# A written-out order for all steps of a chunked RWKV-7 and SiLU kernel, in place of a list scheduler's

## The chip, the cores and the metric

The kernel runs on one core of one Trainium2 chip, as one launch. The time is device microseconds of that core, median over runs. Engines are named as in the profile: PE (TensorE matmul) and PEld (its weight loads), DVE (VectorE), ACT (ScalarE), POOL (GpSimd), SP (SyncE, which issues most of the DMAs).

## The reference

Two blocks follow each other. The first is a recurrence over 768 tokens for 4 batches and 8 heads, with a state of 40 by 40 for each; the second is a feed-forward layer on the recurrence's output.

```python
for t in range(S):                     # r, k, v, w, a, b: (4, 8, 768, 40) float32
    y[:, :, t] = np.einsum('bhd,bhde->bhe', rt, state)
    Sa = np.einsum('bhde,bhe->bhd', state, at)
    state_decay = state * wt[:, :, None, :] - np.einsum('bhd,bhe->bhde', Sa, bt)
    state = state_decay + np.einsum('bhd,bhe->bhde', vt, kt)
x = y.transpose(0, 2, 1, 3).reshape(3072, 320)
h = x @ w_in                           # (320, 2048)
return (h * (1.0 / (1.0 + np.exp(-h)))) @ w_out    # w_out: (2048, 320), both weights float64
```

## The kernel before

The 768 tokens are cut into 12 chunks of 64. Inside a chunk the recurrence is written as products of small matrices and one triangular inverse per head and batch; between chunks only the state `G` is handed on. For chunk n the code lays down groups of steps:

- `load(n)`, `load_r(n)`: DMAs of w, b, a, k, v, and of r and v again.
- `prepare(n)`: on DVE two scans over w (`down`, `up`; L627, L645), the products that make `kb` and `a` (L664, L654); on PE the products of all keys with `a` (`between`, L682), transposes (`turn`, L769) and `sv` (L744); on ACT the copies out of PSUM (`sb` L407, `kt` L782, `R` L756).
- the inverse. For the first three chunks it is `special(n)`: small diagonal blocks go through DRAM (`ms`) to `xs`, DVE inverts them step by step (`dots`, L795 and L796), the result comes back through DRAM (`zs`) to `mi`, and PE and DVE alternate in three rounds (`more`, L958 on PE, L973 on DVE). For the later chunks it is `inverse(k)`, two chunks at a time on DVE, and `merge(n)` (L1039, L1068 on PE).
- `chain(n)`: the state's path. `right` (L1111), `solve` (L1135), `solve_t` (L1166), `turn` (L1196), `update` (L1223), with DVE's L1121 and L1239 between them.
- `read(n)`: the chunk's output y. `look` (L1269) and its masking on DVE (L1281), `write_state` (L1308), `write` (L1323), `scaled` (L1334).
- `moe(n)`: the feed-forward layer on the chunk's 256 rows. `full` (L1405) and `rest` (L1418) fill four PSUM tiles, ACT applies SiLU (L1428), `second` (L1445) multiplies by `w_out`, DVE copies out (L1457).

Once, at the start, `weights(i)` for i from 0 to 9 turns the float64 weights into float32 by bit operations: DMAs from POOL's queue (L479), then steps on DVE (L484, L486, L487, L493, L500), ACT (L485, L488, L502) and, for the first three, sums on PE (`sum_`, L508) and a product on DVE (L520).

Every group calls `plan.add(engine, cost, do, r, w, pri, rooms, k, size, shape)`, which only records a step: its engine, an estimated cost, the steps that it must follow (from the keys it reads and writes), and the PSUM or SBUF tiles ("rooms") that it takes from a small pool, four PSUM tiles `pair` and two SBUF tiles `lam`. There are 1449 steps: 383 on PE, 391 on DVE, 223 on ACT, 21 on POOL, 431 on SP. `shape` is a letter for the form of a PE step's matmuls: F for the full array of 128 by 128 (`full`, `second`, `sum_`), R for `rest`, Q for the 64-wide small products, T for transposes, H for `write` and `update`, S for `merge`.

The order in which the steps are emitted is the order of the instructions in each engine's queue, and each engine takes its queue strictly in that order. `plan.best(10, 400)` searches for it: a list scheduler (`order`) places the steps one by one by estimated times and priorities, a second model (`through`) rates the whole order, and 410 settings of the priorities are tried with a fixed random seed. Then the steps are emitted:

```python
    with tc.manual_schedule():
        for op in plan.best(10, 400):
            op["do"]()
```

Of the kernel before, what the change touches and what calls it, by code (L numbers as in the profile page):

```python
# [33 lines left out]
class Plan:  # L34
# [4 lines left out]
    def __init__(self, slots):  # L39
        self.slots = slots  # L40
        self.free = {k: [(0.0, i) for i in range(len(v))] for k, v in slots.items()}
        self.ops, self.wrote, self.read = [], {}, {}
# [23 lines left out]
    HOP = {"SP": 0.1, "ACT": 0.15, "PE": 0.15, "DVE": 0.15, "POOL": 0.2}  # L66
    RATE, LAND = 300.0, 2.0
    COLD = 42.0
    URGE = {"SP": 0.0, "ACT": 0.03, "PE": 0.05, "DVE": 0.1, "POOL": 0.02}
    LEAVE = {"F": 0.09, "R": 0.2, "T": 0.13, "Q": 0.13, "H": 0.12, "S": 0.11}  # L70
    ENTER = {"F": 0.08, "R": 0.1, "T": 0.03, "Q": 0.03, "H": 0.03, "S": 0.03}

    def turn(self, op):

        a, b = self.shape, op["shape"]
        if a == b or {a, b} == {"R", "T"}:
            return 0.03 if a != "F" else 0.0
        return self.LEAVE[a] + self.ENTER[b]

    def walk(self, start, cost, k, keep=False):  # L80


        fetched, count, t = self.fetched[-2:], self.count, start
        step, end = cost / max(k, 1) * (2 if start < self.COLD else 1), count + k
        have = len(self.fetched)
        while count < end:
            block = count // 256
            gate = 256 * block + 194
            if have == block + 1:
                fetched.append(max(t + 0.4, fetched[-1] + 2.6) + 1.3)  # L90
                have += 1
            if count >= gate:
                t = max(t, fetched[-1] + 0.1)
            to = min(end, gate if count < gate else 256 * block + 256)
            t += (to - count) * step
            count = to
        if keep:
            self.fetched += fetched[2:]
            self.count = end
        return t  # L100

    def order(self):
        ops = self.ops
        self.fetched, self.count, self.shape = [0.0, 0.0], 0, "Q"
        nexts = [[] for _ in ops]
        for op in ops:
            op["wait"] = len(op["before"])
            for b in op["before"]:
                nexts[b].append(op)
        ready = {e: [op for op in ops if op["engine"] == e and not op["wait"]] for e in self.HOP}  # L110
        at = dict.fromkeys(self.HOP, 0.0)
        out, held = [], {}
        queue = dict.fromkeys(("SP", "ACT", "POOL"), 0.0)
        for op in ops:
            op["ready"] = 0.0
        while len(out) < len(ops):
            best = None
            for e, some in ready.items():
                starts = []
                for op in some:  # L120
                    s = max(at[e], op["ready"])
                    for room in op["rooms"]:
                        if room.slot is None:
                            free = self.free[room.kind]
                            fits = free and held.get((room.kind, room.most), 0) < room.most
                            s = max(s, min(free)[0]) if fits else 1e9
                    lost = 0.0
                    if e == "PE" and s < 1e8:
                        lost = self.walk(s + self.turn(op), op["cost"], op["k"]) - s - op["cost"]
# [3 lines left out]
                urge = self.URGE[e]  # L133
# [1526 lines left out]
```

## Time and profile before

| | before |
|---|---|
| median of 3 runs | 734.69 us (729.82 to 736.58) |
| profiled execution | 734.2 us from first to last instruction; no time outside it is shown |
| PE busy, PEld busy | 676.8 us, 542.3 us |
| DVE, ACT, POOL busy | 419.7, 194.1, 15.2 us |
| mean granted PE clock | 0.971 |
| DMA | 77.15 MB, 105 GB/s on average |

The profile gives for each engine how long it was busy, for a stretch of time how much of it each engine was busy and at which share of full speed the PE clock was granted, and for an instruction how long its engine had stood idle before it and what ended the idle time. In a row of the time line, "[4.01 <-PE pair L958]" says that the engine had been idle for 4.01 us and that PE's L958 released it. PE's records are doubled: each matmul of the program in float32 shows as two.

### The profile page before, as it was taken

To read this page: it belongs to the slowest core of one execution; us is meant where nothing else is said; L and a number is where in the kernel's file an instruction comes from. 1 tells how busy PE (TensorE), PEld (TensorE's weight loads), DVE (VectorE), ACT (ScalarE), POOL (GpSimd) and SP (SyncE) were. 2 spreads that over 40 slices of the span, in tenths; PEclk is the share of its full clock that TensorE was granted. 3 is DMA by queue.
4 is the path that set the end of the run, shared out by engine and by line. 5 is a ranking of instruction groups with operands and counts; after the bars stand their busy time and mean duration, and the time that the engine had idled before them with its cause. 6 is when DMAs were issued, how large, how long until landed. Compare 5 with 4: busy or idle time off the path is not lost.

```text
span 734.2 us, 27298 instructions
## 1 busy us (share of the span) xinstructions
PE 676.8 (92%) x12666; PEld 542.3 (74%) x12666; DVE 419.7 (57%) x614; ACT 194.1 (26%) x241; POOL 15.2 (2%) x35
## 2 busy tenths in 40 slices
PE   2179899998999999999999999999999999999995
PEld 2177568787778678878778878778777778787773
DVE  6845799977469348397364883372992676020000
ACT  3251625422302413304312305132104312102020
POOL 2101000000000000000000000000000000000000
PEclk9996999999899999999999999999997999999998
DMA  7680754751721554417355306354215033201001
GB/s 249 150 235 27 205 194 128 223 128 37 177 93 25 137 138 141 126 46 162 81 136 142 103 19 145 87 149 130 66 27 119 26 103 108 44 20 41 18 1 22
DMA packets 117921, 77.15 MB, mean 105 GB/s; under 512 B 65538, under 2 KB 114229, under 8 KB 117160
## 3 DMA queue, kind: packets, MB, share of 16 engines
q1 hardware_dynamic: 113220, 64.43, 33.5%
q0 software_dynamic: 2224, 10.63, 4.4%
q8 instruction: 101, 1.65, 0.9%
q10 hardware_dynamic: 2356, 0.26, 0.3%
q14 instruction: 20, 0.16, 0.1%
HBM read 60.29 MB, written 14.61 MB: 102 GB/s over the span
## 4 chain that ended last, share of the span: by engine, by line
PE 86%; DVE 5%; ACT 3%; issue 2%; DMA 1%; SPq 1%; ACTq 0%; DVEq 0%
PE pair L1445 30%; PE pair L1405 23%; PE pair L1418 6%; PE pair L1269 4%; PE pair L682 3%; PE pair L1323 3%; PE pair L958 2%; PE pair L1223 2%; PE pair L744 2%; PE pair L1135 2%; PE pair L1068 2%; PE pair L1308 1%; PE pair L1111 1%; PE pair L1166 1%; PE pair L508 1%
## 5 line engine op out<-in xcount | busy, mean ns | idle before, releaser
L1445 PE MATMUL pair<-wo,gts 128*128 128x320 f32 x768 | 221.6, 445 | 0.2 <-issue 0.2
L1445 PEld LDWEIGHTS pair<-wo,gts 128*128 128x128 f32 x768 | 145.7, 193 | 60.5 <-issue 4.3
L1405 PE MATMUL pair<-xt,wi 128*128 128x256 f32 x768 | 176.6, 387 | 0.2 <-DVE wi L520 0.2
L1405 PEld LDWEIGHTS pair<-xt,wi 128*128 128x128 f32 x768 | 145.6, 192 | 22.8 <-issue 1.3
L1428 ACT ACTIVATE gts<-pair 128x1024 f32<-128x1024 f32 x48 | 46.5, 1020 | 107.5 <-PE pair L1418 100.4
L1457 DVE COPY ot<-pair 128x320 f32<-128x320 f32 x24 | 11.8, 491 | 95.2 <-PE pair L1445 93.5
L682 PE MATMUL pair<-a,kb 40*64 40x64 f32 x1536 | 33.5, 241 | 33.5 <-DVE a L654 28.7
L796 DVE TENSOR_REDUCE XI<-XI 128x64 f32<-128x512 f32 (+9 forms) x85 | 58.7, 690 | 2.9
L682 PEld LDWEIGHTS pair<-a,kb 40*64 40x64 f32 x1536 | 29.7, 153 | 36.6 <-issue 18.4
L1418 PE MATMUL pair<-xt,wi 64*128 64x256 f32 x384 | 47.9, 389 | 0.0
L1418 PEld LDWEIGHTS pair<-xt,wi 64*128 64x128 f32 x384 | 35.1, 187 | 6.3 <-issue 2.0
L1334 DVE TENSOR_TENSOR lam<-pair,wz 128x1024 f32<-128x1024 f32 x11 | 13.5, 1224 | 41.6 <-PE pair L1323 41.4
L1281 DVE TENSOR_TENSOR lam<-pair,ml 128x1024 f32<-128x1024 f32 x22 | 26.5, 1220 | 14.0 <-PE pair L1269 12.4
L795 DVE TENSOR_TENSOR XI<-XI,mi 128x1024 f32<-128x1024 f32 (+8 forms) x60 | 33.7, 561 | 1.5
L1269 PEld LDWEIGHTS pair<-r,vut 40*64 40x64 f32 x1536 | 26.3, 142 | 6.4 <-issue 4.8
L1269 PE MATMUL pair<-r,vut 40*64 40x64 f32 x1536 | 29.3, 228 | 1.1 <-issue 1.1
L664 DVE TENSOR_TENSOR kb<-kbv 128x512 f32<-128x512 f32 (+1 forms) x36 | 29.8, 860 | 0.2
L1001 ACT COPY mi<-XI 128x1024 f32<-128x1024 f32 x5 | 10.1, 2023 | 70.6 <-DVE XI L796 70.6
L627 DVE TENSOR_TENSOR_SCAN kbv<-wz,zt 128x1024 f32<-128x1024 f32 x12 | 27.5, 2292 | 0.5
L645 DVE TENSOR_TENSOR_SCAN wz<-wz,zt 128x1024 f32<-128x1024 f32 x12 | 27.5, 2291 | 0.4
L795 DVE TENSOR_TENSOR XI<-XI,xs 128x1024 f32<-128x1024 f32 (+1 forms) x25 | 25.2, 1009 | 0.7
L407 ACT ACTIVATE vu<-pair 64x640 f32<-64x640 f32 x13 | 9.1, 700 | 58.8 <-PE pair L1135 56.0
(152 smaller groups left out, 686.8 us busy)
## 6 DMA issues: line engine op xcount, KB each, us to landing
wz<-in_wT SPq DMA_DIRECT2D x12, 512.0 KB
kbv<-in_bT SPq DMA_DIRECT2D x12, 512.0 KB
a<-in_aT SPq DMA_DIRECT2D x12, 512.0 KB
kbv<-in_kT SPq DMA_DIRECT2D x12, 512.0 KB
r<-in_rT SPq DMA_DIRECT2D x48, 96.0 KB
vut<-in_vT SPq DMA_DIRECT2D x48, 96.0 KB
vu<-in_v SPq DMA_DIRECT2D x24, 160.0 KB
out<-ot SPq DMA_DIRECT2D x48, 80.0 KB
```

Source lines behind the costliest of these rows:

```text
L627: nc.vector.tensor_tensor_scan(back(V), back(W[:, 2 : 2 + Q * C]), zt, 1.0, ALU.mult, ALU.add)
L645: nc.vector.tensor_tensor_scan(Z, Z, zt, 0.0, ALU.mult, ALU.add)
L664: TTn[engine].tensor_tensor(out=at_(kb, place(is_b, first), (576 * step, 4 // step), (128, 4), (1, C)), in0=blocks((kf, bf)[is_b]), in1=bl ...
L682: nc.tensor.matmul(room.tile[half(b), j, g * C : g * C + C], lhsT=kb[rows(j), place(is_b, q) : place(is_b, q) + C], rhs=A[rows(j), q * C : ...
L795: nc.vector.tensor_tensor(out=at_(tmp, 0, *dims), in0=x, in1=y, op=ALU.mult)
L796: nc.vector.tensor_reduce(out=out_, in_=at_(tmp, 0, *dims), axis=AX.X, op=ALU.add)
L1269: nc.tensor.matmul(pl.tile[half(1 - b if role else b), b, c * C : c * C + C], lhsT=vut[rows(b), role, hu, :], rhs=rs[rows(b), hh, :], star ...
L1281: lambda pl=pl, la=la: nc.vector.tensor_tensor(out=la.tile.rearrange("p (q t) -> p q t", q=Q), in0=pl.tile.rearrange("p a b -> p (a b)").r ...
L1405: nc.tensor.matmul(rooms[g].tile[:, f // 2, (f % 2) * T : (f % 2) * T + T], lhsT=wi[:, k, (4 * g + f) * 128 : (4 * g + f) * 128 + 128], rh ...
L1418: nc.tensor.matmul(rooms[g].tile[:, h, (f % 2) * T : (f % 2) * T + T], lhsT=wi3[half(h), g * 256 + (f % 2) * 128 : g * 256 + (f % 2) * 128 ...
L1428: nc.scalar.activation(out=gts[:, 4 * g * T : 4 * g * T + 4 * T], in_=rooms[g].tile.rearrange("p a b -> p (a b)"), func=AF.Silu)
L1445: nc.tensor.matmul(po[b].tile[:, 0, 0:DM], lhsT=g4[:, f, 128 * b : 128 * b + 128], rhs=wo[:, f, :], start=f == 0, stop=f == NF - 1,)
```

## The change

`order`, `through`, `best` and their constants are removed. In their place a table, `ORDER`, lists the numbers of all 1449 steps in the order in which they are emitted, and `SLOTS` gives for each room, in the order in which the rooms first appear, which of the four or two tiles it gets. `follow` assigns the tiles, asserts that every step stands behind those that it depends on, and returns the steps.

```diff
-    def order(self):
...
-    def through(self, out, crowd, rate, hop, slower):
...
-    def best(self, draws, steps):
...
+    def follow(self, order, slots):
+
         rooms = {id(room): room for op in self.ops for room in op["rooms"]}
...
+        assert sorted(order) == list(range(len(self.ops))) and len(slots) == len(rooms)
+        for room, slot in zip(rooms.values(), slots):
+            room.slot, room.tile = int(slot), self.slots[room.kind][int(slot)]
+        done = set()
+        for n in order:
+            assert self.ops[n]["before"] <= done
+            done.add(n)
+        return [self.ops[n] for n in order]
+
+ORDER = """
+0 7 3 12 1 8 10 84 2 6 116 9 13 14 11 15 16 24 19 23 20 21 22 17 18 33 34 85 128 90 117 91 92 118 4 86 119 120
...
+SLOTS = """
+03001232301203122111130320222320301111320102321113313310011210213030203110022213111112000230101001222221320121
...
-        for op in plan.best(10, 400):
+        for op in plan.follow([int(n) for n in ORDER.split()], "".join(SLOTS.split())):
```

The steps, their instructions and what each must wait for are the same as before; only their order in each queue and the tiles are other ones. In the changed file every line of the kernel stands 144 lower, so L682 is L538 there, and L1445 is L1301.

Three places show it. The first is DVE in the first chunks, from the last round of `more` for chunk 0 (L973) on. Before, `off_diagonal` of chunk 1 (L900) comes next, and the maskings of `look` for chunk 0 (L1281) stand between the first and the later `dots` of chunk 1 (L795, L796):

```order
L973 TENSOR_TENSOR X_94<-pair_111,X_94 128x4x128
L900 TENSOR_TENSOR sb_90<-sb_90,ml 128x1024
L729 TENSOR_TENSOR lam_116<-pair_113,ml 128x1024
L795 TENSOR_TENSOR XI<-ZQ,xs 128x2
L796 TENSOR_REDUCE ZQ<-XI 128x2
L795 TENSOR_TENSOR XI<-ZQ,xs 128x8
L796 TENSOR_REDUCE ZQ<-XI 128x2x2
L1281 TENSOR_TENSOR a_83<-pair_114,ml 128x1024
L1281 TENSOR_TENSOR sb_89<-pair_113,ml 128x1024
L795 TENSOR_TENSOR XI<-ZQ,xs 128x18
```

Now all `dots` of chunk 1 follow the last round of `more` (L829, once L973) without a break, and this stands behind them, from the last pair of them on:

```order
L651 TENSOR_TENSOR XI<-ZQ 128x512
L652 TENSOR_REDUCE ZQ<-XI 128x8x8
L340 TENSOR_SCALAR wi<-wo 128x2x512
L376 TENSOR_TENSOR wi_67<-wi_67,pair_114 128x1024
L1137 TENSOR_TENSOR sb_89<-pair_113,ml 128x1024
L342 SCALAR_TENSOR_TENSOR wi<-wo,wi 128x2x512
L343 TENSOR_SCALAR wo<-wo 128x1024
L1137 TENSOR_TENSOR a_83<-pair_114,ml 128x1024
L756 TENSOR_TENSOR sb_90<-sb_90,ml 128x1024
```

So the maskings (L1137, once L1281) and `off_diagonal` of chunk 1 (L756, once L900) moved behind the `dots`, and weight steps (L340, L376, L342, L343) stand between them. The masking of chunk 1's `sv` (L729, now L585) and two weight steps moved ahead of the rounds of `more`.

The second place is PE's queue at the start. Before, from the fourth row on, with `prepare` of chunk 1 (L682), `special` of chunk 0 (L926, L913) and `more` (L958); the first weight sum (L508) stands only at row 22:

```order
L769 MATMUL pair_114<-ident,kb 128x40 x16
L744 MATMUL pair_111<-vu_99,lam_115 64x40 x32
L682 MATMUL pair_112<-a_84,kb 64x64 x32
L926 MATMUL pair_113<-ident,mi 128x64 x8
L926 MATMUL pair_114<-ident,mi 128x64 x8
L913 MATMUL pair_111<-mi,sb_89 64x64 x16
```

Now, from the same transpose on (L625, once L769; L769 at the end of these rows was L913):

```order
L625 MATMUL pair_113<-ident,kb 128x40 x16
L538 MATMUL pair_114<-a_83,kb 64x64 x32
L364 MATMUL pair_111<-gts,ident 128x512 x3
L538 MATMUL pair_113<-a_84,kb 64x64 x32
L364 MATMUL pair_111<-gts,ident 128x512
L538 MATMUL pair_112<-a_84,kb 64x64 x32
L769 MATMUL pair_114<-mi,sb_89 64x64 x16
```

The four sums of the first weight block (L364, once L508) and the second product of chunk 1's `prepare` moved ahead of `special`, and `sv` of chunk 0 (L744) moved behind `more`.

The third place is PE's queue in chunk 4's `second` (L1445), where the steps of chunk 5 lie between its parts. Before:

```order
L1445 MATMUL pair_111<-wo,gts 128x320 x4
L1269 MATMUL pair_113<-r,vut 64x64 x32
L769 MATMUL pair_114<-ident,kb 128x40 x16
L1445 MATMUL pair_111<-wo,gts 128x320 x4
L1323 MATMUL pair_112<-lam_115,kt_88 40x64 x16
L1323 MATMUL pair_112<-lam_116,kt_88 40x64 x16
L1039 MATMUL pair_113<-ZQ,sb_89 32x32 x32
L1445 MATMUL pair_111<-wo,gts 128x320 x4
L1068 MATMUL pair_114<-X_94,ZQ 32x32 x32
L682 MATMUL pair_112<-a_84,kb 64x64 x32
L1445 MATMUL pair_111<-wo,gts 128x320 x4
L1445 MATMUL pair_113<-wo,gts 128x320 x8
```

Now, in the same chunk (L1301 was L1445, L1179 was L1323, L538 was L682, L991 was L1135, L625 was L769, L1079 was L1223):

```order
L1301 MATMUL pair_111<-wo,gts 128x320 x4
L1179 MATMUL pair_113<-lam_116,kt_88 40x64 x16
L1179 MATMUL pair_113<-lam_115,kt_88 40x64 x16
L538 MATMUL pair_114<-a_84,kb 64x64 x32
L991 MATMUL pair_112<-R_93,X_95 64x40 x32
L625 MATMUL pair_113<-ident,kb 128x40 x16
L625 MATMUL pair_114<-ident,kb 128x40 x16
L1301 MATMUL pair_111<-wo,gts 128x320 x4
L1301 MATMUL pair_112<-wo,gts 128x320 x4
L1301 MATMUL pair_111<-wo,gts 128x320 x4
L1301 MATMUL pair_112<-wo,gts 128x320 x4
L1079 MATMUL pair_114<-vu_100,kt_88 40x40 x32
```

The small steps stand in longer groups between parts of `second`, and the parts follow each other more often, in turn for the two halves of the chunk's rows. Over the 383 steps of PE, the shape letter changes from one step to the next 242 times before and 205 times now.

More of the change, by code (lines that the diff above doesn't have):

```diff
@@ L3 @@
 from math import prod
-from random import Random
 import concourse.bass as bass
@@ L40, in __init__ @@
         self.slots = slots
-        self.free = {k: [(0.0, i) for i in range(len(v))] for k, v in slots.items()}
         self.ops, self.wrote, self.read = [], {}, {}
@@ L64, in add @@
         return op
[L66 to L100, printed above, removed]
```

177 lines of the change are left out of this document (4 added, 173 removed), and 56 rows, old and new, of the table ORDER.

## The prediction

> **What bounds the kernel now.** I read the page's shares first, then the slices, then the chain that ended last, and then the stretches in which PE is not full.
>
> ```profile
> span 734.2 us, 27298 instructions
> PE 676.8 (92%) x12666; PEld 542.3 (74%) x12666; DVE 419.7 (57%) x614; ACT 194.1 (26%) x241; POOL 15.2 (2%) x35
> PE   2179899998999999999999999999999999999995
> DVE  6845799977469348397364883372992676020000
> PEclk9996999999899999999999999999997999999998
> PE 86%; DVE 5%; ACT 3%; issue 2%; DMA 1%; SPq 1%; ACTq 0%; DVEq 0%
> ```
>
> PE is busy 92% and carries 86% of the chain. From the fifth slice (73 us) on its digits are 8 and 9 alone until the last one. So no other order can gain much there except by making the same matmuls pass faster: fewer breaks between kinds, fewer waits of under a microsecond, fewer windows at a low clock. Before that, in the first slices, PE waits. The kernel has two regimes, and I cost the new order in each.
>
> Stretches of the start, with the busy time of PE, PEld, DVE, ACT and POOL, then clock, DMA share and GB/s:
>
> ```profile
> 0.00:36.00 36.00, 7.43 (x224) 7.11 (x224) 27.29 (x61) 11.25 (x14) 7.67 (x22) 1.00 0.71 200
> 36.00:76.00 40.00, 35.22 (x969) 28.95 (x970) 21.53 (x39) 13.47 (x20) 3.72 (x7) 0.83 0.46 127
> 76.00:102.00 26.00, 23.05 (x376) 15.85 (x376) 20.50 (x24) 11.53 (x11) 1.62 (x3) 1.00 0.59 169
> 102.00:144.00 42.00, 39.28 (x802) 31.39 (x801) 39.75 (x44) 24.23 (x27) 1.06 (x2) 0.96 0.61 197
> ```
>
> From 102 to 144 us DVE is busy 39.75 of 42 us: it decodes the last weights, and PE's `second` of chunk 0 cannot end before the last block is there. So up to 144 us DVE is the bound, and what it idled earlier is what the start costs. That is 8.7 us before 36, 18.5 us from 36 to 76, 5.5 us from 76 to 102 and 2.3 us after, 35 us in all. PE takes its first step of chunk 1's `full` right after:
>
> ```profile
> 150.68 6.91 PE pair L1405 x32
> ```
>
> (The row of the chain starts 0.4 us inside that step.)
>
> **Term 1, the start.** DVE's waits in that stretch:
>
> ```profile
> 20.48 1.23 DVE L900 TENSOR_TENSOR sb<-sb,ml 128x1024 f32<-128x1024 f32 x1 [1.77 <-DMA ms<-sb]
> 43.72 0.69 DVE L973 TENSOR_TENSOR XI<-pair,X 128x512 f32<-128x512 f32 x1 [4.01 <-PE pair L958]
> 47.23 0.69 DVE L973 TENSOR_TENSOR XI<-pair,X 128x512 f32<-128x512 f32 x1 [1.88 <-PE pair L958]
> 54.42 1.23 DVE L900 TENSOR_TENSOR sb<-sb,ml 128x1024 f32<-128x1024 f32 x1 [3.62 <-DMA ms<-sb]
> 61.39 1.23 DVE L1281 TENSOR_TENSOR a<-pair,ml 128x1024 f32<-128x1024 f32 x1 [3.70 <-PE pair L1269]
> 68.78 1.29 DVE L1334 TENSOR_TENSOR X<-pair,wz 128x512 f32<-128x512 f32 x2 [2.16 <-PE pair L1135]
> 72.45 0.82 DVE L1239 TENSOR_TENSOR G<-pair,wc 128x640 f32<-128x640 f32 x1 [0.94 <-PE pair L1223]
> 81.70 1.23 DVE L486 SCALAR_TENSOR_TENSOR wi<-wo,wi 128x1024 int32<-128x1024 int32 x1 [1.52 <-ACT wi L485]
> ```
>
> Each is a step at the head of DVE's queue with work behind it that was ready. In the new queue:
>
> - 4.01 us ahead of the first L973: seven steps now stand there (two L729, L900, L520, L484, L486, L487). At 1.2 us for each of the five long ones and 0.7 for the two short ones (L486 above takes 1.23, L900 1.23) they are 7.4 us of work. The wait goes.
> - 3.62 us at L900: it waited for the DMAs that read `sb`, and held up the `dots` behind it. L900 now stands behind the `dots`. The wait goes.
> - 3.70, 2.16 and 0.94 us: `look` (L1269) and what follows it came late on PE, and DVE stood at their masking. All `dots` of chunk 1 and some weight steps are now ahead of it. The waits go, 6.8 us.
> - 1.77 us at 20 us, and others before 36: `down` of chunk 1 stands directly behind chunk 0's `prepare`, so DVE works while `sb` goes through DRAM. But the wait for `xs` comes back in another form, and I take 2 us as gained.
> - 1.52 us and the like from 76 to 102: I take 1 us of 5.5.
>
> That is 4.0 + 3.6 + 6.8 + 2 + 1 = 17.4 us. The 1.88 us and the small waits between rounds stay: there PE and DVE alternate whatever the queue. Against it stand three `dots` of chunk 2 (about 1.3 us) that moved ahead of the last weight steps, and about 1 us for `write` of chunk 0, whose masking is now later in DVE's queue than `update`. **Term 1: 17.4 - 2.3, some 15 us.**
>
> PE must follow. Two rows say that it can:
>
> ```profile
> 36.16 1.99 PE L682 MATMUL pair<-a,kb 40*64 40x64 f32 x64 [15.07 <-DVE a L654]
> 57.26 2.07 PE L508 MATMUL pair<-gts,ident 128*128 128x512 f32 x2
> ```
>
> PE stood idle for 15.07 us until chunk 1's `a`; the four sums of the first weight block (2.07 us at 57 us) now lie in that gap, and chunk 1's second product follows its first. So after `more` PE has some 10 us less ahead of chunk 0's `update`. What is behind a later instruction matters too: on ACT the second half of chunk 0's `u` (L407) now stands behind a weight step that waits for DVE's `dots`; walked through with the durations above, it comes free about when PE reaches `update`. On SP, one piece of `xt` stands behind the `ms` DMAs of chunk 2, but only `rest` reads it, after two `full` (7.11 us, row below).
>
> Bounds of the term: 24 us if all that DVE idled between 36 and 102 us goes, and 5 us if only the two L900 waits do (1.77 and 3.62) and the others come back elsewhere. I take 15, nearer to the sum of named waits.
>
> **Term 2, fewer changes of form.** Rows of the chain, each a run on PE between two other kinds:
>
> ```profile
> 286.23 3.65 PE pair L1405 x16
> 296.27 7.11 PE pair L1405 x32
> 309.20 17.43 PE pair L1445 x64
> 361.74 2.35 PE pair L1445 x8
> 388.22 1.09 PE pair L1269 x64
> 289.88 2.02 PE pair L1269 x128
> ```
>
> Two L1405 steps in one run take 7.11 us and apart 7.30, so a break costs 0.19. Two L1269 steps: 2.18 - 2.02 = 0.16. Eight L1445 steps in a run take 17.43, 2.18 each, against 2.35 alone: 0.17 to 0.2. From chunk 1's `full` to the end, the shape letter changes 197 times before and 169 times now; 28 x 0.16 = **4.5 us**. The nine other changes lie in the start, where DVE is the bound. Bounds: 3 us at 0.1 for a break that was part hidden, 6 us at 0.2.
>
> **Term 3, the clock.** Stretches at a low clock, in the same columns:
>
> ```profile
> 53.20:66.90 13.70, 13.58 (x288) 10.22 (x290) 7.50 (x18) 1.89 (x3) 0.00 (x0) 0.50 0.06 14
> 131.70:135.20 3.50, 3.50 (x8) 2.06 (x7) 3.47 (x5) 2.72 (x3) 0.00 (x0) 0.51 0.68 183
> 196.60:203.40 6.80, 6.65 (x95) 4.78 (x88) 2.60 (x5) 0.00 (x0) 0.00 (x0) 0.50 0.75 198
> 247.80:251.30 3.50, 3.50 (x32) 1.93 (x31) 0.00 (x0) 0.99 (x2) 0.00 (x0) 0.51 0.60 104
> 558.40:568.70 10.30, 9.49 (x147) 8.12 (x144) 1.39 (x2) 2.44 (x4) 0.00 (x0) 0.50 0.47 89
> ```
>
> The first two are in the start. The other three are 20.6 us at half speed, a loss of 10.3 us. What stood ahead of them:
>
> ```profile
> 195.79 1.25 PE L682 MATMUL pair<-a,kb 40*64 40x64 f32 x60 [0.92 <-issue]
> 246.31 0.69 PE L769 MATMUL pair<-ident,kb 40*128 40x40 f32 x16 [0.81 <-DVE ZQ L409]
> 557.15 0.75 PE L1039 MATMUL pair<-ZQ,sb 32*32 32x32 f32 x64 [0.72 <-DVE lam L729]
> 559.34 1.99 PE L682 MATMUL pair<-a,kb 40*64 40x64 f32 x64 [0.81 <-DVE ZQ L409]
> ```
>
> Small matmuls with gaps of under a microsecond. Counting the steps by their durations, PE has 11 stretches of over 3.4 us after chunk 1's `full` that hold no F or R step, the longest 11.5 us; the new order has 17, the longest 5.5 us. Two of the 11 (190 and 555 us) were followed by half speed, and a shorter stretch (244 us). More stretches but shorter ones: I take nearly the same loss, **2 us** less, with bounds of 10.3 gained and 10.3 lost again.
>
> [...]
>
> **Term 4, waits for other engines.** The waits at 246, 557 and 559 us come from DVE steps that PE reached too soon. In the new order at least one `full`, `rest` or part of `second` (1.9 us and up) lies between `merge`'s two products in nearly all chunks, and between `look` and `write`. I take **2 us**, with bounds of 0 and 3.
>
> "issue" waits of near 1 us, like the 0.92 above, come where small matmuls are densest: counted over PE's records, those at 168, 172, 196, 353, 357, 391 and 496 us come 194 or 195 instructions past a multiple of 256. The new order has about as many places where 256 instructions pass in under 2.4 us. Nothing, with 4 us to either side.
>
> **The sum.** 15 + 4.5 + 2 + 2 = 23.5 us from 734.2 us, 710.7 us. The median is 0.5 us above the profiled execution, so 711 us. Outside the profile nothing is added or removed: the last stretch is the same steps.
>
> **The rivals.**
>
> - *The start gains little.* The in-order queues of ACT and SP hold what DVE's queue no longer does: the L407 behind a weight step, `xt` behind the `ms` DMAs. Then term 1 is 5 us, and the time is 711 + 10 = 721, with 720 to 728 around it. For it speaks that ACT's queue has such a crossing; against it that ACT is busy only 13.47 of the 40 us from 36 to 76.
> - *The clock stays full* after the start: term 3 is 10.3 us in place of 2, and the time 711 - 8.3 = 702.7, down to 698 with the upper bound of term 2 and some of the "issue" waits gone. For it: no stretch is longer than 5.5 us. [...]
> - *Half speed in most chunks*, which is the way to a slower kernel. The 17 stretches of small steps are spread over all chunks. If one of them is followed by a phase like that at 558 us, it costs 10.3 / 2 = 5.1 us. Without any the time is 702.7, so six such phases bring back the time before, and the eighth, at 743 us, makes it slower by over 1%. Against it: of the 11 stretches before, only two had such a phase, and each held a gap of 0.8 us or more.
> - *Nothing measurable*: the waits move and the sum stays within 1%. The order rows leave no doubt that the queues change, so this needs terms that cancel.
>
> **How the numbers follow.** The forecast, 703 to 720 us, gets 0.68; the start that gains little 0.13; the full clock 0.12; half speed in most chunks 0.04; nothing measurable 0.03. A measurement of this kernel, whose runs lie between 729.82 and 736.58 us, tells about 1% from no change, so faster means under 727.3 us: 0.68 + 0.12 + 0.11 of the first rival, 0.91. Same gets 0.05, slower 0.04. The range goes from 698, the full clock with the bounds of terms 1 and 2 partly reached, to 727, the upper end of the rival on the start.
>
> **What would show it.** In the changed profile: the first `full` of chunk 1 (then L1261) at 133 to 138 us instead of 150; DVE idle some 20 us up to there instead of 35; L756 and L1137 without waits of 3 us; half speed after the start for about 18 us in all; single waits of PE for DVE after 150 us under 0.5 us. It is wrong if the start ends later than 145 us, which would show an ACT or SP crossing that I judged too small, or if phases at half speed add up to over 40 us.

## The result, and the profile after

| | before | after |
|---|---|---|
| median | 733.28 us (729.82 to 737.61, 9 runs) | 742.85 us (739.27 to 745.82, 9 runs) |
| ratio | | 1.0108 (95%: 1.0072 to 1.0144) |
| profiled execution, span | 734.2 us | 737.7 us (739.51 us with what lies around it) |

The change makes the kernel slower by 1.1% by the ratio, where 711 us was forecast, and the time lies above the predicted range of 698 to 727 us. The medians are 9.6 us apart, 1.3%; all ratios here are those on record for the fast runs, and are not quotients of the medians. The page of the changed kernel, with the rows that answer to those of before:

```profile
span 737.7 us, 27220 instructions
PE 672.7 (91%) x12666; PEld 543.0 (74%) x12666; DVE 417.9 (57%) x614; ACT 194.0 (26%) x241; POOL 16.2 (2%) x35
PE   2597989999999998999999999999999999999995
DVE  7769787984876454926275854356962454511000
PEclk9879979999999999999999999989999999999998
q8 instruction: 101, 1.65, 0.9%
PE 80%; DMA 6%; issue 5%; DVE 4%; SPq 3%; ACT 1%; ACTq 0%; DVEq 0%
```

PE's work is the same, and from the fifth slice on PE's slices are as full as before. What differs is in the last row. In the chain, DMA went from 1% to 6% and SPq, which issues DMAs, from 1% to 3%. Most of the DMA pieces lie in the start: `ms` and `xs` of chunk 1 (7.85 us from 44 us on, 3.40 from 52), `a` of chunk 2 (9.04 from 74) and v of chunk 1 (8.98 from 94). They belong to the start, which is taken up below. The share of "issue" went from 2% to 5%: in the start it grew from 9.2 to 16.8 us, and in the rest, from PE's step 65 on (see below), from 8.6 to 21.8 us. The waits of PE by what ended them show where that is. Before, from 150 to 725 us (all rows with "issue"; columns: total us, times, longest):

```profile
PE pair L682 <- issue: 2.8, 4, 0.9
PE pair L1269 <- issue: 1.1, 2, 0.6
PE pair L1308 <- issue: 0.9, 1, 0.9
PE pair L744 <- issue: 0.8, 1, 0.8
PE pair L1445 <- issue: 0.2, 1, 0.2
```

After, from 142 to 729 us (the largest six of twelve such rows; the other six add 3.8 us):

```profile
PE pair L1164 <- issue: 4.7, 3, 2.2
PE pair L600 <- issue: 3.7, 2, 2.5
PE pair L1125 <- issue: 2.9, 3, 1.4
PE pair L924 <- issue: 2.7, 3, 1.1
...
PE pair L1179 <- issue: 1.4, 2, 0.9
PE pair L769 <- issue: 1.4, 1, 1.4
```

5.8 us became 20.6 us. All of these waits stand 193 to 195 instructions past a multiple of 256 in PE's records. I take them for waits for the next block of instructions: the row "q8 instruction" above has 101 packets with 1.65 MB, 16 KB each, and PE's queue of 25,449 records (25,332 matmuls and weight loads, the rest its own waits and branches, which count in the position too) is 99.4 blocks of 256. Below they are called **block waits**. One of them on PE's time line in the changed kernel:

```profile
277.74 0.64 PE L625 MATMUL pair<-ident,kb 40*128 40x40 f32 x16
278.31 1.10 PE L1022 MATMUL pair<-X,R 64*40 64x64 f32 x64
279.24 1.09 PE L991 MATMUL pair<-R,X 64*64 64x40 f32 x64
280.14 0.64 PE L600 MATMUL pair<-vu,lam 64*64 64x40 f32 x27
283.24 1.17 PE L600 MATMUL pair<-vu,lam 64*64 64x40 f32 x37 [2.46 <-issue]
```

Three small steps in a row, each about 1 us long and 128 instructions (64 matmuls and their weight loads), and in the third PE stands for 2.46 us, in the middle of a step whose first 27 matmuls have passed. The packets of queue q8 show why. The point "194" is the instruction 194 past a multiple of 256:

```
                        last "194"   block's DMA starts   took    next "194": PE goes on
after, 283 us              278.69         280.74          0.88      283.24   (other DMAs busy 61%)
after, 408 us              404.59         405.33          1.24      408.00   (2%)
after, 572 us              569.01         569.72          1.10      572.10   (2%)
```

There are 22 such waits in this stretch, if gaps down to 0.06 us are counted. In all of them PE goes on 1.2 to 1.6 us after the block has come, and the DMA takes 0.9 to 1.5 us. It starts 0.6 to 1.1 us after the last "194" in fifteen, 1.7 to 2.1 us after it in five, among them the first row, where other DMAs are busy, and 0.3 us or less after it in two (at 627 and 672 us). So 256 instructions took 3.1 to 3.5 us in the fifteen, 4.0 to 4.8 in the five and 2.5 to 2.6 in the two, where PE's own work was 2.0 to 4.4 us. Where the block was there already, PE did not wait: from 428.40 to 430.64 us 256 instructions passed in 2.24 us, and the DMA had ended at 426.38 us.

One PE step can be compared exactly in all kernels here: where both orders have the same set of PE steps behind them. That is so at PE's steps 65, 142 and 381 (of 383). From step 65 to step 381, with every gap of PE over 0.06 us counted and half speed at half its length (at half speed the matmuls of L1301 follow each other in 533 ns in the changed kernel, at full speed in 269 ns, medians):

| worked out from the trace | before | after | difference in time |
|---|---|---|---|
| step 65 reached at | 130.9 us | 127.7 us | -3.2 |
| block waits after it | 6.6 us | 20.6 us | +14.0 |
| other waits of PE | 3.9 us | 2.0 us | -1.9 |
| stretches at half speed | 23.9 us | 20.5 us | -1.7 |
| what is left over (changes of shape: 200, 171) | | | -3.7 |
| time from step 65 to 381 | 590.6 us | 597.3 us | +6.7 |

(The 6.6 us before are the 5.8 us above and a gap of 0.77 us at 181 us, two or three instructions short of such a place. The profile puts it down to DVE, and it ended 0.67 us before the block's DMA did, so that it is a block wait is not shown.)

### The profile page after: what moved, and what is told of

It is laid out like the page before. It is cut to its first block, busy times and chain, and to the rows that moved or that the text cites. A ratio compares the mean times of both kernels' runs of the same rounds, so it can differ in the third digit from the quotient of the medians.

```text
span 737.7 us, 27220 instructions
## 1 busy us (share of the span) xinstructions
PE 672.7 (91%) x12666; PEld 543.0 (74%) x12666; DVE 417.9 (57%) x614; ACT 194.0 (26%) x241; POOL 16.2 (2%) x35
## 3 DMA queue, kind: packets, MB, share of 16 engines
q8 instruction: 101, 1.65, 0.9%
## 4 chain that ended last, share of the span: by engine, by line
PE 80%; DMA 6%; issue 5%; DVE 4%; SPq 3%; ACT 1%; ACTq 0%; DVEq 0%
PE pair L1301 29%; PE pair L1261 22%; PE pair L1274 6%; PE pair L1125 3%; PE pair L538 3%; PE pair L1179 3%; PE pair L1079 2%; PE pair L1164 2%; PE pair L924 1%; PE pair L625 1%; PE pair L600 1%; PE pair L1022 1%; DMA ms<-sb 1%; PE pair L967 1%; DMA a<-in_aT 1%
## 5 line engine op out<-in xcount | busy, mean ns | idle before, releaser
L1301 PE MATMUL pair<-wo,gts 128*128 128x320 f32 x768 | 223.1, 446 | 0.0
L1301 PEld LDWEIGHTS pair<-wo,gts 128*128 128x128 f32 x768 | 146.8, 195 | 59.5 <-issue 4.6
L1261 PEld LDWEIGHTS pair<-xt,wi 128*128 128x128 f32 x768 | 147.5, 194 | 23.8 <-issue 1.1
L1137 DVE TENSOR_TENSOR lam<-pair,ml 128x1024 f32<-128x1024 f32 x22 | 26.3, 1220 | 48.8 <-PE pair L1125 48.8
L538 PE MATMUL pair<-a,kb 40*64 40x64 f32 x1536 | 30.5, 236 | 20.1 <-DVE a L510 20.0
L538 PEld LDWEIGHTS pair<-a,kb 40*64 40x64 f32 x1536 | 27.6, 149 | 25.4 <-ACT kbv L532 14.6
L263 ACT ACTIVATE sb<-pair 128x1024 f32<-128x1024 f32 x12 | 12.3, 1027 | 60.0 <-PE pair L538 48.1
L638 ACT COPY kt<-pair 128x640 f32<-128x640 f32 x24 | 16.3, 693 | 43.8 <-PE pair L625 41.9
L1190 DVE TENSOR_TENSOR lam<-pair,wz 128x1024 f32<-128x1024 f32 x11 | 13.5, 1223 | 21.8 <-PE pair L1179 21.7
```

The source lines that it names most:

```text
L538: nc.tensor.matmul(room.tile[half(b), j, g * C : g * C + C], lhsT=kb[rows(j), place(is_b, q) : place(is_b, q) + C], rhs=A[rows(j), q * C : ...
L1137: lambda pl=pl, la=la: nc.vector.tensor_tensor(out=la.tile.rearrange("p (q t) -> p q t", q=Q), in0=pl.tile.rearrange("p a b -> p (a b)").r ...
L1261: nc.tensor.matmul(rooms[g].tile[:, f // 2, (f % 2) * T : (f % 2) * T + T], lhsT=wi[:, k, (4 * g + f) * 128 : (4 * g + f) * 128 + 128], rh ...
L1301: nc.tensor.matmul(po[b].tile[:, 0, 0:DM], lhsT=g4[:, f, 128 * b : 128 * b + 128], rhs=wo[:, f, :], start=f == 0, stop=f == NF - 1,)
```

## The experiments

Each is the whole kernel; only `ORDER` and `SLOTS` differ, or a few matmuls are added. "Old" is the order before, "new" that of the change. Ratios are to the kernel before on the same chip.

**1. The two orders crossed at step 142.** There the new order was 10.0 us ahead in the profile.

```diff
-ORDER = new
+ORDER = new up to PE's step 142, then the old order for all that is left   (new_then_old)
+ORDER = old up to PE's step 142, then the new order for all that is left   (old_then_new)
```

> The new order for PE's first 142 steps and what goes with them on the other engines, then the old order for the rest. PE has the very same 142 steps behind it at that place in both kernels, and reached it at 266.3 us in the changed profile against 276.3 before: a lead of 10.0 us. Theory 'blocks' (the new order's second part loses because small matmuls stand closer, and PE waits for the next block of 256 instructions): the second part is the old one and keeps its crossings, since the number of PE instructions ahead of it is the same, so the lead stays: 733 - 10 = 723 us, within 3 us. Rival 'debt' (the new start only pushes loads, weight steps and copies back, and pays for them later): the lead is lost again, 733 to 743 us. Rival 'clock' (half-speed phases fall by accident): anything from 715 to 735, by 3.4 us in each phase that appears or goes at half speed for 6.8 us.

> The reverse: the old order for PE's first 142 steps, then the new order. 'Blocks': without the lead and with the dense second part, 10 us above the changed kernel or 13.5 above the one before, 747 to 750 us; block waits of over 15 us after 277 us. 'Debt': the old start leaves nothing to pay, so the second part costs what it cost before, 730 to 736 us. 'Clock': between the two, with the phases at half speed elsewhere.

Measured: 736.70 us, ratio 1.0026 (0.9979 to 1.0073), and 751.29 us, ratio 1.0261 (1.0159 to 1.0364). The second time lies just above the 747 to 750 us that "blocks" gave, and the block waits after step 142 are 15.1 us, over 15 as expected. But it is no proof, because the crossing itself brings a wait that neither order has. At step 142 PE stood for 7.89 us, until DVE had the `a` of a `prepare` that it had begun only then:

```profile
277.70 1.98 PE L537 MATMUL pair<-a,kb 40*64 40x64 f32 x64 [7.89 <-DVE a L509]
```

Half speed went with it from 272.2 to 285.8 us. PE worked for 8.1 of these 13.6 us, which costs some 4 us. With both taken off, 751 us would be some 739, between the 730 to 736 of "debt" and the 747 to 750 of "blocks". The first run does not agree with "blocks", and its time lies in the range of "debt". PE came to step 142 at 268.7 us, 7.6 us ahead, and the old second part then lost it again: 9.0 us of block waits against 2.9 in the old kernel's own profile, mostly at the same steps, and 20.5 us at half speed against 10.2. One block's DMA started 2.5 us after PE had entered the block before, and PE waited for 3.1 us. So the same order pays different block waits in different executions, and a lead of 10 us in one pair of profiles is not a lead of the median. This pair of runs does not decide between "blocks" and "debt"; experiments 2, 3 and 5 do.

**2. A shift in the blocks.** Matmuls of the identity are added where PE is idle; every later step then lies further on in its block.

```diff
+                    if sums.pop('left', 0):
+                        for d in range(10):      # 48 in the other run
+                            px, py = slice(64 * (d % 2), 64 * (d % 2) + 64), slice(64 * (d // 2 % 2), 64 * (d // 2 % 2) + 64)
+                            nc.tensor.matmul(pf.tile[py, d % 2, 0:64], lhsT=ident[px, px], rhs=ident[px, px], start=True, stop=True)
                     nc.tensor.matmul(
                         pf.tile[:, h],
```

> The changed kernel with 10 matmuls of 64 by 64 (40 PE instructions, under 1 us) ahead of the first weight sum, where PE stands idle. Nothing else moves, but each later step lies 40 instructions further in the 256-instruction blocks. 'Blocks': taking the profiled stream of the changed kernel with its block waits removed, and letting each crossing come no sooner than 3.0 to 3.3 us after the one before, the waits after 142 us come to 13 to 19.5 us as it is (20.6 measured) and to 19.6 to 26.5 with 40 more: some 6.5 us slower than the changed kernel, 747 to 751 us. 'Debt' and 'clock': as the changed kernel, 739 to 746, with the waits at the same steps.

> As the last, with 48 matmuls (192 instructions, under 3 us in PE's idle time of 3.9 us). 'Blocks': by the same sum the waits come to 9.7 to 14.7 us, some 4 to 5 us less: 736 to 740 us, and some 12 us less than with 40. 'Debt' and 'clock': as the changed kernel, 739 to 746.

Measured: 734.85 us, ratio 1.0041 (0.9989 to 1.0093) with 40 instructions, and 727.37 us, 0.9907 (0.9863 to 0.9952) with 192. By the ratios that is 0.7% and 2.0% less than the changed kernel's 1.0108, some 5 and 15 us. The interval of the first overlaps the changed kernel's, that of the second does not. That 48 idle matmuls take 15 us out of the kernel is what "debt" and a fixed cost of the order cannot give; PE came to step 65 no earlier than in the changed kernel, so the gain lies behind it. My sizes were wrong, though: with 40 I had the sign wrong. The block waits after step 65 were 15.7 and 12.0 us (after: 20.6) and half speed 6.8 and 10.2 us (20.5). The first is under my sum of 19.6 to 26.5, because I let each crossing take 3.0 to 3.3 us, where the profile has some that wait for nothing: at 428 us of the changed kernel, above, the 256 instructions before had taken 13.0 us, and the block's DMA had ended 2.0 us before the 2.24 us began.

**3. The dense groups opened.** At 13 places of the new order one step of the full array moves ahead of the last small step of a group. The place of the time line above, on PE:

```diff
 L1022 MATMUL pair<-X,R x32
 L991 MATMUL pair<-R,X x32
+L1261 MATMUL pair<-xt,wi x8
 L600 MATMUL pair<-vu,lam x32
-L1261 MATMUL pair<-xt,wi x8
 L1261 MATMUL pair<-xt,wi x8
```

> The changed kernel's order, with one step of the full array (`full` or `second`) moved ahead of the last small step of a dense group, at 13 places behind chunk 1's first `full` where PE had waited 194 instructions past a multiple of 256. Every other queue keeps its order. 'Blocks': each 194th instruction then comes 3.0 us or more after the last one, and by the sum over the profiled stream the block waits fall from 20.6 us to 3 to 7; 18 more changes of shape at 0.16 us cost 2.9 us; of the half speed behind the longest waits (20.5 us) a third to a half goes, 3 to 5 us gained. 743 - 15 + 3 - 4 = 727 us, within 5. Rival 'breaks' (the prediction's own model, in which only the changes of shape count): 743 + 3 = 746 us. Rival 'debt' (the start pays back later): 743, no change.

Measured: 726.46 us, ratio 0.9888 (0.9838 to 0.9937), where 727 was expected and 746 by the prediction's own model. The same place (the lines stand one lower here):

```profile
281.83 1.10 PE L1021 MATMUL pair<-X,R 64*40 64x64 f32 x64
282.76 1.09 PE L990 MATMUL pair<-R,X 64*64 64x40 f32 x64
283.78 3.72 PE L1260 MATMUL pair<-xt,wi 128*128 128x256 f32 x16
287.43 1.14 PE L599 MATMUL pair<-vu,lam 64*64 64x40 f32 x64
289.39 3.72 PE L1260 MATMUL pair<-xt,wi 128*128 128x256 f32 x16 [0.81 <-ACT R L611]
```

The wait of 2.46 us is gone; a smaller one for ACT is the price. And from the eighth slice (127 us) on, no slice is under nine tenths of full clock, and the trace has no half speed between 127 us and the end of the work at 723 us:

```profile
PE   1488797998999999999999999999999999999995
PEclk9888998999999999999999999999999999999999
```

From step 65 to 381 this kernel takes 579.2 us, 18.1 less than the changed one: block waits 3.2 instead of 20.6 us, half speed 0 instead of 20.5 us (10.2 us of time), other waits 9.2 instead of 2.0, and 2.4 us left over for 18 more changes of shape, 0.13 each. The steps that I had counted as a gain, fewer changes of shape, are here given up with profit. That the time came out at 727 almost to the microsecond is partly luck: half speed gave back 10.2 us where 3 to 5 were expected, and the other waits took 7.2 us that were not in the sum.

**4. DMAs of r and v earlier.** Seven loads move ahead of DMAs at which SP stood.

```diff
 L448 DMA r<-in_rT 48x2x256
+L448, L457 DMA r, vut (the other seven of chunk 1)
 L555 DMA ms<-sb 16x16x16 x2
-L457, L448 (seven, between the next DMAs)
```

> The changed kernel with seven DMAs of r and v for chunk 1 moved ahead of the two DMAs of chunk 2's small blocks, at which SP stood from 76 to 88 us. In the changed profile PE waited 2.87 us for v at 103 us, in `look` of chunk 1, and 10.2 us at half speed followed, 5.1 us lost. 'SP queue': both go, chunk 1's first `full` comes at 134 to 139 us in place of 141.7, and the end with it, 735 to 740 us. Rival 'DVE bounds the start': PE then waits for DVE's weights instead, and nothing is left of it by 150 us: 741 to 745.

> Both of the last two edits. If both work by themselves, their gains add: 743 - 16 - 5 = 722 us, within 6, faster than the kernel before. If the loads do nothing, as with the 13 moved steps alone.

Measured: 743.54 us, ratio 1.0116 (1.0058 to 1.0173), and with the opened groups 729.03 us, 0.9964 (0.9924 to 1.0005). PE's wait for v went, and nothing was gained. The time is the rival's, but not its cause: from 80 to 152 us PE's longest waits were not for DVE's weights but block waits, 3.21 us at 93 us and 4.45 us at 115 us in the first of the two. The start ended no earlier; step 65 came at 134.5 and 134.3 us.

**5. The wait measured by itself.** Two trains of matmuls that wait for nothing, at the start and behind all work.

```diff
+    for d in range(640):
...
+        nc.tensor.matmul(pairs[0][py, d % 2, 0:64], lhsT=ident[px, px], rhs=ident[px, px], start=True, stop=True)
+    for d in range(320):
...
+        nc.tensor.matmul(pairs[0][py, d % 2, 0:128], lhsT=ident[px, px], rhs=ident[px, 0:128], start=True, stop=True)
     nc.tensor.matmul(pb[0:1, 0:1], lhsT=count, rhs=ones, start=True, stop=True)
```

> The changed kernel with two trains of matmuls that nothing waits for, once ahead of the first weight sum (DMAs busy) and once after all work (DMAs idle): 640 matmuls of 64 by 64 by 64, 2560 PE instructions, and 320 with 128 columns, 1280 instructions. At the profiled rate of 15.6 ns for a pass of 64 columns the first train takes 20 us, 2.0 us for each 256 instructions. 'Blocks': PE waits once in each 256 instructions and passes them in 3.0 to 3.4 us with the DMAs idle and up to 4 us with them busy, 30 to 40 us for the train; the second train, at twice the time for an instruction, has 4 us for each 256 and no waits. Rival (the waits come from tiles, semaphores or loads): no waits in either train, 20 us each. Nothing of the kernel's work is left out.

PE's time line behind all work, with the DMAs idle (128 records are 256 instructions with their weight loads):

```profile
777.46 2.09 PE L1383 MATMUL pair<-ident 64*64 64x64 f32 x128 [1.04 <-issue]
780.93 2.09 PE L1383 MATMUL pair<-ident 64*64 64x64 f32 x128 [1.38 <-issue]
784.67 2.09 PE L1383 MATMUL pair<-ident 64*64 64x64 f32 x128 [1.65 <-issue]
788.69 2.09 PE L1383 MATMUL pair<-ident 64*64 64x64 f32 x128 [1.93 <-issue]
...
811.49 16.89 PE L1386 MATMUL pair<-ident 64*64 64x128 f32 x591 [1.05 <-issue]
```

and in the start, with the DMAs busy:

```profile
24.83 2.10 PE L369 MATMUL pair<-ident 64*64 64x64 f32 x128 [0.46 <-issue]
31.03 3.69 PE L369 MATMUL pair<-ident 64*64 64x64 f32 x128 [4.10 <-issue]
38.05 3.69 PE L369 MATMUL pair<-ident 64*64 64x64 f32 x128 [3.33 <-issue]
```

256 instructions are 2.09 us of work, and PE waits once in each 256, but for one block of the start at half speed: a block takes 3.1 to 4.0 us with the DMAs idle and 3.1 to 7.0 with them busy. With 128 columns a block passes in 3.5 to 3.8 us, and 591 records pass without a wait of over 0.15 us. Tiles, semaphores and the kernel's loads of data have no part in the waits with idle DMAs. (The whole kernel with its trains took 837.31 us, in a single run.)

**6. The start, and the form.** The old start before the opened new order; the old order as a table; the load of chunk 2's `a` earlier; and two dense groups of the start opened as well.

```diff
+ORDER = old up to PE's step 65, then the new order with the 13 moved steps   (old_start_spread)
+ORDER = old                                                                   (old_table)
+ORDER = 13 moved steps; L421 DMA a<-in_aT of chunk 2 right behind L421 wz<-in_wT   (spread_early_a)
+ORDER = the last; L967 of chunk 1 behind the last L814, L1164 behind one L1261     (spread_start)
```

> The old order for PE's first 65 steps and what goes with them, then the new order with the 13 moved steps. PE has the same 65 steps behind it there in all of these kernels. It came there at 130.9 and 126.4 us in the two profiled executions that begin with the old order, and in the seven that begin with the new one at 126.5, 127.7, 130.9, 131.0, 134.3, 134.3 and 134.5. Theory 'the start gains nothing': the time is that of the 13 moved steps with the new start, 726, or up to 5 us less, 721 to 727. Rival 'the start gains its 15 us' (term 1 of the prediction): without the new start the time is 741. Rival 'a few us', as the first pair of profiles has it (3.2): 730.

> The old order and the old tiles, written out as a table: nothing but the form of the change, without its order. 'The form costs nothing': the time before, 731 to 736 us, and the profile a second sample of the old order's waits, block waits of 6 to 12 us after 150 us. If the form mattered, or if the two versions differed in anything but the order, it would lie elsewhere.

> The new order with the 13 moved steps, and one DMA more moved: the load of chunk 2's `a` (0.5 MB) stands on SP right behind that of w, three loads and a few small DMAs earlier. In the seven profiled executions of the new start DVE stood at the step that reads this `a` for 0.7, 0.9, 1.7, 4.0, 5.6, 6.3 and 6.7 us, with all work behind it waiting. 'A load at the head of DVE's queue eats the start's gain': that wait goes, and the time falls from 726.5 to 721 to 725 us. Rival 'other loads take its place' (the DMAs are full from 78 to 86 us, so that k and b come later by what `a` gains): 726 to 728, with a wait at the steps that read k and b.

> As spread_early_a (13 moved steps, the load of `a` earlier), with two more steps moved on PE in the start, where its waits were longest in the profile: chunk 1's `right` stands behind the last `more`, where PE waited 2.68 us at 86 us, 194 instructions past a multiple of 256, in the middle of a round between PE and DVE; and `write_state` of chunk 1 stands behind one `full`, where PE waited 2.58 us at 111 us. 'Blocks also in the start': the first wait falls where PE waits for DVE anyway, and the second behind a step of 3.6 us; with less half speed behind them PE reaches its step 65 at 124 to 128 us in place of 130.6, and the ratio to before goes from 0.987 to 0.980 to 0.985. Rival 'the start is bound by DVE and its loads': the waits go and others take their place, ratio 0.987, step 65 at 130 us or later.

Measured: 731.82 us, 0.9895 (0.9828 to 0.9961); 736.76 us, 0.9962 (0.9915 to 1.0009); 729.88 us, 0.9874 (0.9814 to 0.9934); 725.85 us, 0.9812 (0.9773 to 0.9851). The table as a form costs nothing. The old start is as good as the new one (0.9895 against 0.9888; the times in us are not to be compared, since the kernel before took 738.81 us on the chip of the first and 732.59 on that of the second). What the new start waits for, on DVE in the changed kernel, in experiment 3 and with the earlier load:

```profile
83.31 1.23 DVE L510 TENSOR_TENSOR a<-a,wz 128x1024 f32<-128x1024 f32 x1 [0.73 <-DMA a<-in_aT]
```

```profile
89.42 1.23 DVE L509 TENSOR_TENSOR a<-a,wz 128x1024 f32<-128x1024 f32 x1 [6.74 <-DMA a<-in_aT]
```

```profile
81.24 1.23 DVE L828 TENSOR_TENSOR XI<-pair,X 128x1024 f32<-128x1024 f32 x1 [3.23 <-PE pair L813]
82.38 1.21 DVE L509 TENSOR_TENSOR a<-a,wz 128x1024 f32<-128x1024 f32 x1
```

The wait for the load goes when its DMA is issued earlier, but the ratio hardly moves, and PE's block waits stay where PE and DVE alternate (spread_early_a):

```profile
85.88 2.72 PE L813 MATMUL pair<-XI 64*64 64x64 f32 x46 [2.68 <-issue]
...
111.41 1.30 PE L1163 MATMUL pair<-r,GT 40*40 40x64 f32 x39 [2.58 <-issue]
```

With these two groups opened (spread_start) they are 0.42 and 0.73 us, and nothing:

```profile
85.75 0.97 PE L537 MATMUL pair<-a,kb 40*64 40x64 f32 x50 [0.42 <-issue]
...
89.48 1.01 PE L966 MATMUL pair<-G,a 40*64 40x40 f32 x51 [0.73 <-issue]
...
112.38 1.10 PE L1163 MATMUL pair<-r,GT 40*40 40x64 f32 x64
```

PE then comes to its step 65 at 127.0 us instead of 130.6, in one profile each, and the kernel has the lowest ratio of all here, 1.9% faster than before. Its interval still overlaps that of spread_early_a, so the gain by these two moves alone is not shown.

The profiled executions side by side, from the trace as in the table above:

```
                  step 65   to 381   block   other   half speed
before             130.9    590.6      6.6     3.9      23.9
old_table          130.1    592.7     11.3     4.6      13.7
after              127.7    597.3     20.6     2.0      20.5
new_loads          134.5    600.5     22.3     1.2      23.9
new_then_old       126.5    599.6     14.9     3.2      27.3
old_then_new       126.4    608.3     18.5    10.3      34.1
new_shift40        130.9    583.5     15.7     0.4       6.8
new_shift192       131.0    581.2     12.0     1.0      10.2
new_spread         134.3    579.2      3.2     9.2       0.0
new_spread_loads   134.3    584.4      6.8     9.5       3.4
old_start_spread   125.5    592.2      5.0    15.1      10.2
spread_early_a     130.6    586.6      7.4     9.6       6.8
spread_start       127.0    586.5      6.0    10.6       6.8
```

## Why the prediction was wrong

**The "issue" waits: this step failed.** The prediction put them at nothing, with 4 us to either side, since "the new order has about as many places where 256 instructions pass in under 2.4 us". They are 14.0 us of loss. Two things were wrong in it. The count: by the traces, stretches of 256 instructions with under 2.4 us of PE work are 7 before and 13 after, from chunk 1's `full` on. And the limit: the 2.4 us were my estimate, which no run shows; 20 of the 22 blocks with a wait above took 3.1 us or more, and stretches of 2.9 to 3.1 us of work wait too (0.30 us at 471 us, 0.48 at 301 and 0.38 at 395). Of the stretches with under 3.3 us of work 20 of 22 had such a wait after the change, and 7 of 16 before. I had the waits at 194 and 195 in hand, and did not ask what sets their length.

The kernel before says more than I read in it. `walk` and `through`, which the change removes, hold back PE at instruction 194 of each block until a modelled fetch has ended (`gate = 256 * block + 194`), and the search chose the old order by these models. That this is why the old order had fewer such waits is likely, but no run here tests it.

What the crossings cost is 20.6 us here, and 1.04 to 1.93 us for each of the nine waits of the 64-column train behind all work.

**Term 1, the start (15 us), failed too.** In the one pair of profiles it is 3.2 us, and that was luck: the seven executions that begin as the new order does, four of them with extra matmuls or moved loads, came to step 65 at 131.3 us on average (126.5 to 134.5), the four that begin as the old one at 128.2 (125.5 to 130.9). So the start gained nothing, and may have cost some 3 us; with 8 us between executions of the same start that is not certain. The waits that I named did go: neither L756 nor L1137 waits 3 us in the start. But DVE's idle time up to chunk 1's first `full`, which I had at 20 us instead of 35, is 28.8:

```profile
0.00:36.00 36.00, 12.15 (x231) 8.92 (x231) 26.74 (x61) 12.91 (x15) 6.24 (x19) 0.93 0.67 191
36.00:76.00 40.00, 33.90 (x908) 25.93 (x906) 32.34 (x54) 19.16 (x25) 4.39 (x7) 0.85 0.54 144
76.00:102.00 26.00, 23.07 (x594) 19.75 (x590) 22.05 (x24) 11.86 (x12) 3.93 (x6) 1.00 0.73 231
102.00:142.00 40.00, 38.17 (x582) 30.84 (x583) 32.05 (x47) 16.80 (x20) 0.53 (x1) 0.87 0.54 163
```

Idle are 9.3, 7.7, 4.0 and 8.0 us. The first `full` came at 142 us, not at 133 to 138, and with less work ahead of it than before. What I did not cost is what the moved steps wait for: `prepare` of chunk 2 now stands ahead of weight steps in DVE's queue, and DVE stood there for its `a` for 0.7 to 6.7 us in seven executions; it also stood 3.6 us for `xs` of chunk 1 and 2.2 us for k; on SP seven loads of r and v, of which the prediction names none, stood behind the `ms` DMAs; and PE had block waits there, 1.58 us at most in the changed kernel's profile but up to 4.45 us in later ones. Experiment 4 shows that the loads of r and v alone were not the limit. In experiment 6 step 65 came 3.6 us earlier with two of the block waits opened, but that is less than the scatter between executions. What the start's loss is made of stays open.

**Term 2 (4.5 us) held within its bounds, and was the wrong thing to want.** What is left over in the table, 3.7 us, lies in 3 to 6; it is 0.13 us for each of the 29 changes of shape, not 0.16, and only what remains when all else is taken off. Where small steps follow each other without a break, they can also pass faster than their blocks come: in the 64-column train of experiment 5, with the DMAs idle, 256 instructions are 2.09 us of work and took 3.1 to 4.0 us.

**Term 3, the clock (2 us), held in size,** 1.7 us in this pair. But I had taken it as an accident of the order. In the 13 profiles of the last listing, 39 phases at half speed lie after the start. All of them set in at a wait of PE of 0.5 us or more, or less than 2 us behind it, 28 at a block wait, all five of the changed kernel among them. All 9 waits over 2 us had such a phase, 7 of them block waits; of 50 between 1 and 1.5 us only 11 had one. The granted clock changes in steps of 3.41 us in these traces: between two changes lie 3.41 us (160.55 to 163.97 us in the changed kernel) or a whole multiple of it, up to 90 times (before). Of such steps at full clock after 150 us, all 13 in which PE was busy under half of the time were followed by half speed, 25 of the 126 with 50 to 80%, and none of the some 1930 with more. How a wait falls on these steps therefore seems to matter: the 2.46 us at 283 us lie in one of them, from 280.02 to 283.43 us, in which PE was busy for 0.95 us. This wait thus cost twice, 2.46 us and 1.7 us for the 3.41 us at half speed behind it, and opening the groups took both (experiment 3: 17.4 us of block waits and all 20.5 us at half speed). The windows at 283 us, ahead of the phase and in it:

```profile
277.00:283.40 6.40, 3.94 (x193) 3.62 (x189) 2.50 (x10) 2.53 (x3) 0.00 (x0) 1.00 0.49 138
283.40:286.80 3.40, 3.40 (x43) 2.87 (x40) 3.16 (x9) 2.32 (x3) 0.00 (x0) 0.50 0.03 7
```

**Term 4, other engines (2 us), held:** 1.9 us, and after 142 us no wait for DVE is left among PE's waits.

In the pair of profiles the changed kernel is 3.5 us longer: 3.2 us earlier at step 65, and 6.7 us more from there on. The medians are 9.6 us apart. With the averages of the start, 3.1 us later, the sum is 9.8 us, but that it meets the medians so closely is luck: the 6.7 us are from one pair, and executions of one kernel lie 8 us and more apart. The rival that gave the start little (0.13) was right in that, but its 720 to 728 us lack the block waits. The rival that ended slower (half speed in most chunks, 0.04) had the cause wrong but one right thing: small steps close together can cost more than they save (14.0 us of block waits against 3.7 us). Neither sign that I gave for a miss (a start beyond 145 us, over 40 us at half speed) came; "issue" in the chain was not on my list.

What stays open is why the same order pays 6.6 us of block waits in one execution and 11.3 in another. Other DMAs seem to be part of it: in the changed kernel they were busy 44 to 100% of the time between the last "194" and the start of the block's DMA where that took 1.7 to 2.1 us, and at most 14% in ten of the fifteen where it took 0.6 to 1.1. In the other five of these it was 42% and more, so they are not all of it.

## What to carry to other kernels

Before grouping small matmuls, count instructions: where 256 of them took PE less than 3.3 us, the next block was late in 20 of 22 places here, and a step of large matmuls between them cost less than the wait (18.1 us less from step 65 to 381, with the other waits and the changes of shape counted). A wait called "issue" is worth placing in PE's records: after the start all of them came 193 to 195 instructions past a multiple of 256 here, and each of the seven over 2 us had 3.4 us or more at half clock with it. When code with a cost model is taken out, read what the model held. When a step moves forward in an in-order queue, look up when its loads are issued, and compare more than one profiled execution before taking a few microseconds of a start for a gain.

## What the runs showed of the hardware

- In the train behind all work, with the DMAs idle, the block's DMA starts 0.8 to 1.2 us after PE has passed the last point 194, takes 0.9 to 1.4 us, and PE goes on 1.3 to 1.5 us after it has come. With busy DMAs it started up to 4.6 us after that point (31.03 and 35.67 us in the first train).
- Waits of up to 1.93 us in each 3.5 to 4.0 us left the clock at full speed for 34 us in the train, with PE busy 57% of the time:

```profile
774.00:808.00 34.00, 19.40 (x1206) 18.25 (x1201) 0.00 (x0) 0.00 (x0) 0.00 (x0) 1.00 0.04 9
```

- 48 matmuls of the identity in an idle place took 2.0% off the changed kernel, some 15 us, by where the blocks fall; ten of them 0.7%, with intervals that overlap.
